# Attention with routed experts on one core: the second half's key sums, moved ahead of the keys' projection

## Chip, cores and metric

The kernel runs on one core of one Trainium2 chip. The metric is the device time of one execution in microseconds (us). Before the change it is 638.71 us, the median of 3 runs (638.54 to 640.49).

## What is computed

The reference is an attention with random features, followed by a mixture of eight experts of which each token uses one (cut):

```python
def _attn_ref(q, k, v, omega):            # 8 batches x 8 heads, 576 tokens, 64 wide; 128 features
    def phi(x):
        h = np.einsum('bhsd,md->bhsm', x, omega) - np.sum(x * x, axis=-1, keepdims=True) / 2.0
        h = h - np.max(h, axis=-1, keepdims=True)
        return np.exp(h) / np.sqrt(m)
    q_p, k_p = phi(q * scale), phi(k * scale)
    kv = np.einsum('bhsm,bhsd->bhmd', k_p, v)
    z = np.sum(k_p, axis=2)
    num = np.einsum('bhsm,bhmd->bhsd', q_p, kv)
    den = np.einsum('bhsm,bhm->bhs', q_p, z)[..., None] + 1e-06
    return num / den

def _moe_ref(x, expert_emb, tau, w1, w2): # 4608 tokens x 512, 8 experts
    ...
    expert_idx = np.argmax(logits, axis=1)
    for e in range(E):
        h = np.maximum(x[mask] @ w1[e], 0.0)
        out[mask] = gate_w[mask, None] * (h @ w2[e])
```

## The kernel before

The work has two stages. The **attention stage** (about the first 220 us) goes through 36 tiles of 128 tokens (`NTILE`), all 8 heads at once; the main loop is `for i in range(NTILE + LAG + 2)`. In its steady part, i = 7 to 35, one iteration handles the keys of tile i and the queries of tile iq = i - 7 (`LAG`), and finishes work of the tiles just before. The **expert stage** (about 220 us to the end) multiplies gathered tokens by expert weights, in products that run one behind the other on TensorE (line 285).

All five engines run in the order in which the program issues its work (`tc.manual_schedule`), so the order of the calls in the loop body is the order on each engine. The heads are kept in two halves a = 0 and a = 1, the lower and the upper 64 partitions of a key or query tile. The helpers that matter here, with their lines:

- `proj` (L374): features before the exponential, for two halves in turns: 8 matmuls into two PSUM banks. The queries go to banks pb3 and pb1, the keys to pb2 and pb0. In the rows its tile form is 64\*128 (64 rows of the array by 128 columns).
- `maxima` (L378, VectorE): the negated row maxima of a bank, `nmk` for keys, `nmq` for queries.
- `feats` (L388, ScalarE): four exponentials, which read the bank and write `ftk` or `ftq`. A bank can be projected into again once its four are done.
- `kvmm` (L406): the key sums of one half, values and counts, 8 matmuls of form 128\*64 into an accumulator `kva`, which collects over the tiles of half a block of tokens. `kv(1)` and `kv(0)` call it for the keys of tile i - 1. `kv_out` (L420, ScalarE) copies finished accumulators to `kvs`, after which they are begun again.
- `qtr` (L462): 16 transposes of the query features into the two banks `nuu`, form 64\*128 like the projections.
- `qcopy` (L467 ScalarE, L469 VectorE): those transposes to SBUF as `qp`.
- `num` (L482): query features times key sums into `nuu`, 32 matmul records of form 128\*64. `num_out` (L495 to L501, VectorE) divides and writes `xr`; `qtr` of the next iteration waits for it, since it writes the same banks.
- `kv_turn`, `kv_turned`, `kv_logits` (L433, L437 VectorE, L444): every fourth or fifth iteration the key sums are transposed and multiplied by the experts' vectors.
- `routed` (L517 to L570): every three tiles the routing, with scatters of rows by GpSimd (L570), one an iteration.

The steady body on TensorE is: query projection, query transposes, key projection, `kv(1)`, `num`, `kv(0)`, and then the next iteration. A value `u` is the tile's place in its block of nine; at u = 4, `kv(0)` and `kv_out` stand directly behind `kv(1)`.

Of the kernel before, what the change touches and what calls it, by code (L numbers as in the profile page):

```python
# [64 lines left out]
def attention_moe(ctx: ExitStack, tc: tile.TileContext, qT, kT, v1, omT, emb, tau, w1q, w2q, xs, out):  # L65
# [114 lines left out]
    def written(w):  # L180

        for o in put + got:
            tc.declare_no_dep(w.ins, o.ins.name, reason="other rows")
        put.append(w)
# [138 lines left out]
    with ExitStack() as c1:  # L323
# [412 lines left out]
        def go(d, *key):  # L736
            for f, *a in d.pop(key, ()):
                f(*a)
# [7 lines left out]
        for i in range(NTILE + LAG + 2):  # L746
            iq = i - LAG
            for n in QLOADS.get(i, () if i >= NTILE else (iq + 2,) if i >= LAG else (i - 4,)):
                loadq(n)
            ahead = i + (4 if i < 2 else 2)  # L750
            if i == 1 or i > 4:
                load(ahead)
            if i in LOADS:
                first_weights(LOADS[i])
            if i == 1 or i >= 4:
                loadv(4 if i == 1 else ahead)
            if i == 1:
                loadv(LAG - 2)
            go(early, i)
            if i == LAG:  # L760
                written(nc.sync.dma_start(xs[DUM : DUM + P, 0:PAY], padrow))
            if i == XLOAD:
                prow = [nc.values_load(
                    firsti[0:1, t : t + 1], engines=[ET.SP], min_val=t * P, max_val=(E - 1) * REG + t * P,
                    skip_runtime_bounds_check_because=WHY) for t in range(NPRE + 1)]
                for t in range(NPRE):
                    xload(t, prow[t], xgp[t])
            ks, qs = i < NTILE, 0 <= iq < NTILE
            st["both"] = ks
            sb, u = divmod(i - 1, TPS)  # L770

            def kv(*halves, b=None):
                if 0 <= i - 1 < NTILE:
                    for a in halves:
                        kvmm(i - 1, a, int(u > 4) if b is None else b)

            turns, done = 0 <= iq - 1 < NTILE, iq - 1 if ks else iq - 2
            sums = 0 <= done < NTILE and i != NTILE
            k0, q1, k1, q0 = ("k", i, 0), ("q", iq, 1), ("k", i, 1), ("q", iq, 0)
            slot = lambda k: go(mid, i, k)  # L780
            if ks and qs:
                if i > LAG:
                    proj(q1 + (3,), q0 + (1,))
                if turns:
                    qtr(iq - 1, *nu)
                maxima(*q1)
                if turns:
                    qcopy(iq - 1, 1)
                    qcopy(iq - 1, 0, True)
                maxima(*q0)  # L790
                go(spare, i, 4)
                feats(*q1)
                feats(*q0)
                proj(k1 + (2,), k0 + (0,))
                maxima(*k1)
                maxima(*k0)
                kv(1)
                if u == 4:
                    kv(0)
                    kv_out(sb, 0)  # L800
                go(spare, i, 3)
                slot(4)
                if sums:
                    num(iq - 1)
                go(spare, i, 0)
                go(spare, i, 1)
                slot(2)
                if u == 4:
                    kv(0, 1, b=1)
                else:  # L810
                    kv(0)
                if sums:
                    num_out(iq - 1)
                feats(*k1)
                feats(*k0)
                slot(0)
                slot(1)
            elif ks:
                for j in KPROJ.get(i, ()):
                    proj(*keys(j))  # L820
                if i == LAG - 1:
                    proj(("q", 0, 1, 3), ("q", 0, 0, 1))
                go(spare, i, 0)
                maxima(*k0)
                maxima(*k1)
                slot(0)
                if i == LAG - 1:
                    kv_out(0, 0)
                    kv_dense(0, 0)
                    for a in range(2):  # L830
                        kvmm(i - 2, a, 1)
                    kv(0, 1)
                    kv_turn(0, 0)
                    emb2()
                else:
                    kv(0, 1)
                slot(1)
                feats(*k0)
                go(spare, i, 1)
                feats(*k1)  # L840
                slot(2)
            else:
                mine, other = ((3, 1), (0, 2))[:: 1 if i % 2 == NTILE % 2 else -1]
                if qs:
                    proj(q1 + (mine[0],), q0 + (mine[1],))
                kv(1)
                go(spare, i, 2)
                slot(3)
                if turns:
                    qtr(iq - 1, *(pb[k] for k in other))  # L850
                kv(0)
                if sums:
                    num(done)
                go(spare, i, 0)
                if i == NTILE + 1:
                    flush()
                if qs:
                    maxima(*q1)
                    maxima(*q0)
                if i > NTILE and turns:  # L860
                    qcopy(iq - 1, 0, True)
                if qs:
                    feats(*q1)
                if i == NTILE:
                    kv_out(sb, 1)
                    qcopy(iq - 1, 0, True)
                if qs:
                    feats(*q0)
                if turns:
                    qcopy(iq - 1, 1)  # L870
                if sums:
                    num_out(done)
                flush()
                filled(1)
                slot(0)
                slot(1)
                filled(FILLS[i] - 1)
                go(spare, i, 1)
                slot(2)
            if sums and done % G == G - 1:  # L880
                g = done // G
                steps = routed(g)
                if g == GPICK:
                    plan = [(ends, i), (mid, i + 1, 2), (mid, i + 1, 1), (spare, i + 2, 0), (mid, i + 2, 0)]
                    plan += [(mid, i + 3, 2), (mid, i + 3, 1)] + [(ends, i + 3 + k) for k in range(3)]
                elif g == NTILE // G - 2:
                    plan = [(ends, i), (ends, i + 1), (ends, i + 1), (spare, i + 2, 0), (mid, i + 2, 0), (mid, i + 2, 1)]
                    plan += [(ends, i + 2), (ends, i + 3), (ends, i + 3)]
                elif i >= NTILE:
                    plan = [(ends, i)] * 3 + [(spare, i + 1, 0), (mid, i + 1, 0), (mid, i + 1, 1)]  # L890
                    plan += [(ends, i + 2 + k) for k in range(3)]
                else:
                    plan = [(ends, i), (mid, i + 1, 2), (mid, i + 1, 1), (spare, i + 2, 0), (mid, i + 2, 0)]
                    plan += [(mid, i + 3, 2)] + [(ends, i + 3 + k) for k in range(3)]
                if NTILE - 3 < i < NTILE:
                    plan[-3:] = [(ends, i + 3), (mid, i + 4, 3), (ends, i + 5)]
                for n, (d, *key) in enumerate(plan):
                    todo = at(d, *key) if key[0] < NTILE + LAG + 2 else behind
                    todo.insert(0 if n == 0 else len(todo), (next, steps, None))
            go(ends, i)  # L900
            if 0 <= i - 1 < NTILE and u in (4, 8):
                b = u // 4 - 1
                if b and ks:
                    kv_out(sb, b)
                k = int(not ks)
                if i + 2 == LAG:
                    todo = (kv_turned, spare, i + 2, 4), (kv_logits, spare, i + 2, 3), (kv_logits_out, mid, i + 2, 4)
                else:
                    kv_dense(sb, b)
                    todo = (kv_turn, spare, i + 2, 3 - k), (kv_turned, mid, i + 2, 4 - k)  # L910
                    todo += (kv_logits, spare, i + 2 + k, 0), (kv_logits_out, mid, i + 2 + k, 0)
                for f, *key in todo:
                    at(*key).append((f, sb, b))
            if i in LOADS:
                n = LOADS[i]
                at(ends, i + 1).append((first_split, n))
                at(early, i + 2).append((first_rest, n))
# [450 lines left out]
```

## Time and profile before

| | before |
|---|---|
| median of 3 runs | 638.71 us |
| the profiled execution: its time | 639.0 us |
| the profiled execution: its span | 637.4 us |
| TensorE (PE) busy | 626.5 us (98%), 6289 matmul records |
| weight loads (PEld) busy | 534.8 us (84%) |
| VectorE (DVE) busy | 499.4 us (78%) |
| ScalarE (ACT) busy | 434.5 us (68%) |
| GpSimd (POOL) busy | 423.1 us (66%) |
| granted TensorE clock, mean | 0.998 |

The end of a matmul in the profile is modelled, so that TensorE looks busy through short pauses; its pauses are better read from the distance between the starts of two neighbouring groups. The time of the profiled execution is 1.6 us above its span, which is what lies ahead of the first and behind the last instruction.

### The profile page before, as it was taken

How to read it: one execution, taken by the hardware profiler on the slowest of the kernel's cores; microseconds unless marked ns; L12 is line 12 of the kernel's file. 1: busy time of each engine (PE TensorE's matmuls, PEld its weight loads, DVE VectorE, ACT ScalarE, POOL GpSimd, SP SyncE). 2: the span in 40 equal slices, each digit the busy share in tenths (PEclk: the TensorE clock that was granted, in tenths of full speed). 3: DMA queues.
4: the chain of work that ended last, by engine and by line, in shares of the span. 5: the costliest groups of instructions: out<-in, count | busy, mean ns of one | idle time of the engine just before them, and what ended most of it. 6: DMA issues, size and time to landing. Idle time of an engine off the chain costs nothing.

```text
span 637.4 us, 19063 instructions
## 1 busy us (share of the span) xinstructions
PE 626.5 (98%) x6289; PEld 534.8 (84%) x6290; DVE 499.4 (78%) x909; ACT 434.5 (68%) x1143; POOL 423.1 (66%) x603
## 2 busy tenths in 40 slices
PE   9999999999999999999999999999999999999996
PEld 8999999988878787888888888888888888888885
DVE  5788888898879846789888798877778787878754
ACT  6989898898998417666666666666575757576640
POOL 3013333455777644569897898879797988797952
PEclk9999999999999999999999999999999999999999
DMA  7755665777782278888869687887878786968631
GB/s 256 216 153 170 210 197 177 226 206 235 250 284 87 101 236 296 249 214 242 244 193 230 208 225 231 201 248 185 242 186 222 216 242 196 234 206 225 195 116 47
DMA packets 143264, 132.20 MB, mean 207 GB/s; under 512 B 107766, under 2 KB 107894, under 8 KB 143168
## 3 DMA queue, kind: packets, MB, share of 16 engines
q1 hardware_dynamic: 136544, 109.96, 61.4%
q0 software_dynamic: 6480, 20.91, 8.4%
q8 instruction: 57, 0.93, 0.6%
q14 instruction: 39, 0.32, 0.2%
q10 hardware_dynamic: 144, 0.07, 0.0%
HBM read 83.78 MB, written 21.97 MB: 166 GB/s over the span
## 4 chain that ended last, share of the span: by engine, by line
PE 70%; ACT 2%; DVE 1%; DMA 1%; issue 0%; POOL 0%; ACTq 0%
PE pb L285 31%; PE po L285 31%; PE pb L374 2%; PE fs_o L285 2%; PE nuu L482 2%; PE fs_a L285 1%; PE pb L267 1%; ACT ftq L388 1%; PE kva L406 1%; DMA qt<-qT 1%; PE pb L462 0%; PE nuu L462 0%; ACT sq L296 0%; DVE xr L501 0%; DVE rt_p L299 0%
## 5 line engine op out<-in xcount | busy, mean ns | idle before, releaser
L240 POOL TENSOR_TENSOR w2l<-raww,w2h 128x256 f32 x128 | 143.6, 1122 | 7.6
L240 POOL TENSOR_TENSOR w1l<-raww,w1h 128x256 f32 (+1 forms) x130 | 114.9, 884 | 14.6 <-DMA xgp<-xs 5.3
L285 PE MATMUL po<-w2h,hh 128*128 (+1 forms) x288 | 112.2, 390 | 0.0
L285 PE MATMUL po<-w2h,hl 128*128 (+1 forms) x288 | 112.1, 389 | 0.0
L285 PE MATMUL po<-w2l,hh 128*128 (+1 forms) x288 | 112.0, 389 | 0.0
L285 PE MATMUL pb<-w1h,xh 128*128 (+1 forms) x280 | 109.4, 391 | 0.1
L285 PE MATMUL pb<-w1h,xl 128*128 (+1 forms) x280 | 109.1, 390 | 0.0
L285 PE MATMUL pb<-w1l,xh 128*128 (+1 forms) x280 | 109.0, 389 | 0.0
L1086 DVE COPY pl<-pb 128x512 uint16<-128x512 uint16 x68 | 46.7, 690 | 55.9 <-ACT pl L1082 53.0
L1082 ACT ACTIVATE pl<-pb 128x512 uint16<-128x512 uint16 x68 | 39.4, 582 | 69.5 <-PE pb L285 61.1
L388 ACT ACTIVATE ftq<-pb,nmq 128x128 f32<-128x128 f32 x288 | 79.7, 432 | 2.2 <-DVE nmq L378 2.2
L388 ACT ACTIVATE ftk<-pb,nmk 128x128 f32<-128x128 f32 x272 | 76.6, 492 | 4.9 <-DVE nmk L378 4.9
L315 POOL DMA_INDIRECT y<-xgp,tail x36 | 44.6, 1240 | 52.0 <-DVE w1h L234 25.3
L1104 DVE COPY wd<-t 128x1024 uint16<-128x1024 uint16 x68 | 67.3, 991 | 1.6 <-DMA t<-pl 1.5
L1120 ACT ACTIVATE hh<-wd 128x1024 fp32r<-128x1024 f32 x34 | 36.1, 1062 | 42.1 <-DVE wd L1104 37.4
L285 PEld LDWEIGHTS po<-w2h,hh 128*128 128x128 f32 x288 | 54.1, 188 | 11.3
L285 PEld LDWEIGHTS po<-w2h,hl 128*128 128x128 f32 x288 | 54.0, 187 | 11.3
L285 PEld LDWEIGHTS po<-w2l,hh 128*128 128x128 f32 x288 | 54.1, 188 | 11.0
L285 PEld LDWEIGHTS pb<-w1h,xl 128*128 128x128 f32 x280 | 52.6, 188 | 11.2 <-DVE xl L269 0.2
L285 PEld LDWEIGHTS pb<-w1h,xh 128*128 128x128 f32 x280 | 52.5, 187 | 11.1 <-ACT tail L1148 0.5
L285 PEld LDWEIGHTS pb<-w1l,xh 128*128 128x128 f32 x280 | 52.6, 188 | 10.8
L1124 DVE SCALAR_TENSOR_TENSOR hl<-wd,hh 128x1024 fp32r<-128x1024 f32 x34 | 54.8, 1611 | 2.9 <-ACT hh L1120 2.3
(342 smaller groups left out, 1257.2 us busy)
## 6 DMA issues: line engine op xcount, KB each, us to landing
raww<-w1q SPq DMA_DIRECT2D x38, 512.0 KB
raww<-w2q SPq DMA_DIRECT2D x38, 512.0 KB
qt<-qT SPq DMA_DIRECT2D x36, 256.0 KB
kt<-kT SPq DMA_DIRECT2D x35, 256.0 KB
xg<-xs SPq DMA_DIRECT2D x23, 260.5 KB
xgp<-xs SPq DMA_DIRECT2D x15, 260.5 KB
rf<-w1q SPq DMA_DIRECT2D x4, 512.0 KB
rf<-w2q SPq DMA_DIRECT2D x4, 512.0 KB
```

What stands on the lines that cost most here:

```text
L240: ils.append(eng.tensor_tensor(at(l, d)[:, c], raw[:, c], at(h, d)[:, c].bitcast(F32), op=ALU.subtract))
L267: nc.tensor.transpose(bank[:, c * P : (c + 1) * P], src[:, o + c * P : o + (c + 1) * P], ident)
L285: done.append(nc.tensor.matmul(dst, x[:, c * P : (c + 1) * P], ws.rearrange("p o f -> p (o f)"), start=(begin and i == 0 and k == 0), stop ...
L315: w = nc.gpsimd.indirect_dma_start(out=out, out_offset=bass.IndirectOffsetOnAxis(ap=(xg[:, DM:] if tail is None else tail)[:, E : E + 1].b ...
L374: nc.tensor.matmul(st["pj" + w, i, a][:, c, :], st[w, i][r, c, :], om[r, :], start=True, stop=True)
L388: nc.scalar.activation(ft[:, h, :], pj[:, h, :], AF.Exp, bias=nm[:, h : h + 1])
L482: nc.tensor.matmul(pn[a][s * D : s * D + D, h, :], st["qp", i, s][:, 2 * h + a, :], kvs[sb, int(u > 4 - s)][:, 4 * a + h, :], start=True, ...
L1082: nc.scalar.activation(planes[1][:, o : o + 512], halved(src)[:, :, 1], AF.Copy)
L1086: nc.vector.tensor_copy(planes[0][:, o : o + 512], halved(src)[:, :, 0])
L1104: nc.vector.tensor_copy(to, src)
L1120: nc.scalar.activation(hh, wd[:, 0:F], AF.Relu)
L1124: nc.vector.scalar_tensor_tensor(hl, wd[:, 0:F], 0.0, hh.bitcast(F32), op0=ALU.max, op1=ALU.subtract)
```

## The change

One call moves three lines up: in iterations 7 to 35, `kv(1)` stands between the query features (behind the query transposes on TensorE) and the key projection, where it stood behind that projection.

```diff
                 go(spare, i, 4)
                 feats(*q1)
                 feats(*q0)
+                kv(1)
                 proj(k1 + (2,), k0 + (0,))
                 maxima(*k1)
                 maxima(*k0)
-                kv(1)
                 if u == 4:
                     kv(0)
                     kv_out(sb, 0)
```

On TensorE, in iteration 8 (`vt7v` and `ftk_1` are the values and the second half's key features of tile 7; `pb_73` and `pb_71` the banks of the key projection; `qp` the query features that `num` multiplies):

```order
 L462 MATMUL nuu<-ident,ftq_1_547 128x64 x2
+L406 MATMUL kva_1_1_490<-vt7v,ftk_1_594 64x65 x8
 L374 MATMUL pb_73<-om,kt_459 128x128
 L374 MATMUL pb_71<-om,kt_459 128x128
...
-L406 MATMUL kva_1_1_490<-vt7v,ftk_1_594 64x65 x8
 L482 MATMUL nuu<-kvs_0_440,qp_0_638 64x73
 L482 MATMUL nuu<-kvs_0_440,qp_1_636 64x73
```

The key sums went from between the key projection and `num` to between the query transposes and the key projection; `num` now follows the projection directly.

On TensorE in iteration 10, where an accumulator is begun anew (with what each instruction waits for; `Activation` is ScalarE):

```order
 L462 MATMUL nuu<-ident,ftq_1_752 128x64 x2
-L374 MATMUL pb_73<-om,kt_606 128x128 [waits DMAHW5_49,Activation_49]
-L374 MATMUL pb_71<-om,kt_606 128x128 [waits Activation_49]
+L406 MATMUL kva_0_1_875<-vt9v,ftk_1_814 64x65 [waits DMAHW2_49,PE_49,Activation_49]
+L406 MATMUL kva_0_1_875<-vt9v,ftk_1_814 64x65 x7
+L374 MATMUL pb_73<-om,kt_606 128x128 [waits DMAHW5_49]
+L374 MATMUL pb_71<-om,kt_606 128x128
```

The wait for ScalarE is now that of the key sums, ahead of the projection, and the projection behind it has none of its own left. Iterations 19 and 28 read the same.

On TensorE in iteration 11, one of those with the transposed key sums (L433):

```order
 L374 MATMUL pb_73<-om,kt_716 128x128
 L374 MATMUL pb_71<-om,kt_716 128x128
-L406 MATMUL kva_0_1_887<-vt10v,ftk_1_928 64x65 x8
 L433 MATMUL pb_74<-ident,xgp_141 128x128 x4
 L482 MATMUL nuu<-kvs_0_440,qp_0_980 64x73
```

The transposes of the key sums now stand directly behind the projection. The rows of VectorE, ScalarE, GpSimd and of the DMA queue on SyncE stand in the order in which they stood.

## Rows read from the trace of the kernel before

**Rows 1.** Busy by stretch: bounds, length, PE, PEld, DVE, ACT, POOL, clock, DMA, GB/s

```profile
20.00:180.00 160.00, 158.57 (x3518) 146.29 (x3516) 137.18 (x326) 142.41 (x512) 67.04 (x191) 1.00 0.68 204
220.00:632.00 412.00, 411.37 (x1838) 339.74 (x1837) 316.46 (x457) 247.70 (x494) 321.15 (x313) 1.00 0.75 214
```

**Rows 2.** The chain that ended last, 160 to 240 us: start, length, what

```profile
180.06 3.63 DMA qt<-qT
```

**Rows 3.** Timeline of PE, iteration 35 and the next: start, length, operation, idle before

```profile
174.01 1.16 PE L374 MATMUL pb<-om,qt 64*128 64x128 f32 x16
175.13 0.71 PE L462 MATMUL nuu<-ident,ftq 64*128 64x64 f32 x16
175.68 1.11 PE L374 MATMUL pb<-om,kt 64*128 64x128 f32 x16
176.72 0.69 PE L406 MATMUL kva<-vt34v,ftk 128*64 128x65 f32 x16
177.24 1.20 PE L482 MATMUL nuu<-kvs,qp 128*64 128x73 f32 x32
...
178.83 1.16 PE L374 MATMUL pb<-om,qt 64*128 64x128 f32 x16
179.92 0.69 PE L406 MATMUL kva<-vt35v,ftk 128*64 128x65 f32 x16
180.66 0.71 PE L462 MATMUL pb<-ident,ftq 64*128 64x64 f32 x16
181.30 0.69 PE L406 MATMUL kva<-vt35v,ftk 128*64 128x65 f32 x16
```

**Rows 4.** Timeline of PE, end of iteration 15 and iteration 16

```profile
65.90 0.69 PE L406 MATMUL kva<-vt14v,ftk 128*64 128x65 f32 x16
66.52 1.16 PE L374 MATMUL pb<-om,qt 64*128 64x128 f32 x16
67.51 0.70 PE L462 MATMUL nuu<-ident,ftq 64*128 64x64 f32 x16
68.06 1.57 PE L374 MATMUL pb<-om,kt 64*128 64x128 f32 x16
...
71.84 0.65 PE L444 MATMUL nuu<-enbd,xgp 128*64 128x16 f32 x16
```

**Rows 5.** Groups by line, PE, 20 to 180 us: busy, mean ns, idle before

```profile
L374 PE MATMUL pb<-om,kt 64*128 64x128 f32 x464 | 37.2, 283 | 0.3 <-ACT ftk L388 0.3
...
L406 PE MATMUL kva<-vt31v,ftk 128*64 128x65 f32 x64 | 2.3, 225 | 0.6 <-ACT kvs L420 0.6
```

**Rows 6.** Timeline of PE, then of ACT, iteration 19

```profile
84.24 0.70 PE L462 MATMUL nuu<-ident,ftq 64*128 64x64 f32 x16
...
84.91 0.79 ACT L420 ACTIVATE kvs<-kva 128x260 f32<-128x260 f32 x2
```

**Rows 7.** The same pair, iteration 10

```profile
35.46 0.71 PE L462 MATMUL nuu<-ident,ftq 64*128 64x64 f32 x16
...
35.80 0.79 ACT L420 ACTIVATE kvs<-kva 128x260 f32<-128x260 f32 x2
```

**Rows 8.** Timeline of DVE, iterations 16 and 8

```profile
71.09 0.69 DVE L437 COPY xgp<-pb 128x512 f32<-128x512 f32 x1 [0.30 <-PE pb L433]
...
29.25 0.17 DVE L495 TENSOR_SCALAR rr<-nuu 128x8 f32<-128x8 f32 x1 [0.21 <-PE nuu L482]
```

**Rows 9.** Timeline of PE, iteration 21

```profile
97.48 0.69 PE L406 MATMUL kva<-vt20v,ftk 128*64 128x65 f32 x16
98.19 1.25 PE L482 MATMUL nuu<-kvs,qp 128*64 128x73 f32 x32
```

**Rows 10.** Timelines of POOL, PE and ACT, iteration 18

```profile
79.04 0.98 POOL L570 DMA_INDIRECT xs<-xr,posi  x1 [0.94 <-DVE sel L530]
...
78.82 0.71 PE L462 MATMUL nuu<-ident,ftq 64*128 64x64 f32 x16
...
80.42 0.60 ACT L467 ACTIVATE qp<-nuu 128x512 f32<-128x512 f32 x1 [0.90 <-PE nuu L462]
```

## The prediction

> **What bounds the kernel.** I read the busy times by stretch first, then the chain that ended last, then the timelines of TensorE against ScalarE and VectorE in single iterations. From 20 to 180 us, where the changed iterations lie, TensorE shows 158.57 of 160 us busy, at full clock, with ScalarE at 142.41 and VectorE at 137.18 [rows 1]: TensorE paces the loop, and two engines are close behind. The expert stage is TensorE alone (411.37 of 412 us). So a microsecond that the loop gains or loses is one of the whole. Where the loop ends, the chain leaves TensorE for a load of queries, issued at 180.06 [rows 2]; the projection that freed its buffer had started at 178.83 and lasted 1.16 [rows 3], so that load starts later if the loop ends later and covers nothing. I carry the loop's difference through in full.
>
> TensorE's modelled ends hide two sorts of pause. One is a **stall of the key projection**: 1.57 us long in iteration 16 [rows 4] against 1.11 in iteration 35 [rows 3], because it writes a bank that ScalarE's last exponentials of the previous keys still read. The other is a **change of tile form**. Projections and query transposes have the form 64\*128, key sums and `num` 128\*64. Where the form stays, neighbours overlap: the key projection starts 0.55 after the transposes (175.13 to 175.68), `num` 0.52 after the key sums (176.72 to 177.24). Where it changes, the next starts later: key sums 0.64 after transposes (180.66 to 181.30) [rows 3], a projection 0.62 after key sums (65.90 to 66.52) [rows 4].
>
> **The change, part by part.**
>
> *Order.* The key sums are moved out of a row of like form into the middle of another, so that an iteration has four changes of form instead of two. Before, from the transposes to `num`: 0.55 + 1.04 + 0.52 = 2.11 [rows 3]. After, from the same view: transposes to key sums 0.64, key sums to projection 0.62, and a projection entered from key sums and left to key sums 1.09 (178.83 to 179.92), taken for the unseen step from projection to `num`, which has the key sums' form: 2.35. `num` itself lasts 1.20 when it follows key sums at once [rows 3] and 1.25 when its stream starts afresh [rows 9]. Together 0.24 + 0.05 = 0.29, in 29 iterations **+8.4**. The bounds: at least the bare difference 0.64 - 0.55 = 0.09 for each of two added changes, 29 x 0.18 = +5.2; at most, if the unseen step cost another such 0.09, +11.0. I take 8.4, since all but that one step is a row.
>
> [...]
>
> *Stalls.* The key projections are busy for 37.2 us and idle ahead of them for 0.3 [rows 5]; 29 at 1.11 would be 32.2, so stalls are 37.2 + 0.3 - 32.2 = 5.3 us. With the key sums ahead, a projection comes 0.64 + 0.62 = 1.26 after the transposes instead of 0.55, 0.71 later, and the stall of 0.46 in iteration 16 is covered. The key sums need only the second half's features, which ScalarE makes before the first half's. **-5.3**. They now wait for each head's exponential by itself; those are done by then, so I cost these waits at nothing. The key tile's buffer comes free 0.7 later, which its next load, more than an iteration ahead of its use, covers.
>
> *A new wait.* In iterations 10, 19 and 28 the key sums begin an accumulator anew and must wait for ScalarE to copy the old one out (L420), and the key projection now stands behind that wait. In iteration 19 they could start at 84.24 + 0.64 = 84.88; the copies end at 84.91 + 0.79 = 85.70, a wait of 0.82 [rows 6]. In iteration 10 it is 36.59 - 36.10 = 0.49 [rows 7]; I take 28 like 10. That makes 1.8, less 0.3 in each of 10 and 28, since the iteration before has made TensorE later by its 0.29 and ScalarE not: **+1.2** (bounds 0 to 1.8).
>
> *Late maxima.* VectorE takes the key maxima behind the key projection. That ends at 175.68 + 1.11 = 176.79 in iteration 35 and would end at 175.13 + 1.26 + 1.16 = 177.55; in stalled iteration 16 at 69.63 before, 67.51 + 2.42 = 69.93 after. So these maxima come 0.3 to 0.8 later. In the iterations with transposed key sums VectorE had 0.30 idle before the copy L437 [rows 8], behind which L444 waits (71.84, rows 4 show it starting as that copy ends, 71.09 + 0.69 = 71.78). There the 0.46 - 0.29 that TensorE wins is lost again: 5 iterations x 0.2 = 1.0. In plain ones only 0.21 was idle before `num_out` [rows 8]; I estimate that 0.1 more than TensorE's own delay reaches the next transposes, in seven of them, 0.7. Iteration 32 wins nothing from its filled stall, since behind it TensorE waits 0.6 for ScalarE anyway [rows 5]; half of that I give back, 0.3. **+2.0** (bounds 0 to 4).
>
> *Cover.* Where `num` waits for the query copies, the added time is partly free: in iteration 21 it starts 0.71 after the key sums [rows 9] instead of 0.52. Where the transposes wait for VectorE too: 1.12 after the query projection in iteration 35 (174.01 to 175.13) [rows 3] against 0.99 in 16 (66.52 to 67.51) [rows 4]. I estimate eight such places at 0.16: **-1.3**.
>
> **Sum.** 8.4 - 5.3 + 1.2 + 2.0 - 1.3 = **+5.0**. The profiled execution took 639.0 us with a span of 637.4; it becomes 644.0. The median is 0.3 below it (638.7), so I forecast 643.7. A measurement tells about 0.3% (1.9 us) from no change.
>
> **The rivals.**
> - *No change.* VectorE and ScalarE keep up: the new wait and the late maxima cost nothing, leaving 8.4 - 5.3 - 1.3 = +1.8, 640.5; with the changes of form at their lower bound 5.2 it is -1.4, 637.3. For it: both engines are idle about a tenth of the loop. Against it: their idle time does not lie at these places [rows 6, 8]. Chance 0.16.
> - *Faster.* The weight loads of the next group slip under the running matmuls in the new order too, and a change of form costs what the like-form step shows beyond the stream itself, some 0.06 an iteration: 1.7 - 5.3 - 1.3 = -4.9, 633.8. It decides itself at the step from transposes to key sums: at 0.55 instead of 0.64 this case holds. All the steps that I see speak against it. Chance 0.05.
> - *Much slower.* In iteration 18 a GpSimd scatter runs from 79.04 to 80.02; the transposes end inside it at 79.53, but ScalarE's copy, released by them, starts only at 80.42 [rows 10]: the release came 0.4 after the scatter's end. If the key projection's end, now later, falls into the scatter of the iterations that follow such a one, and is held alike, VectorE gets its maxima about 1.0 later in seven iterations: +7 on top, 650.7. Against it: that end would fall only some 0.3 into the scatter, and I see no projection held. A partial hold is in my range. Chance 0.12.
>
> The forecast's own case has the remaining 0.67.
>
> **Numbers.** Its own range is 640.5 to 647 (order cost 5.2 to 11.0, not at both ends with the rest). The range that leaves out little over 1 in 10 is 639.2 to 648.5. Slower by over 0.3% (above 640.6): the main case almost whole, the much slower one, and a little of the first rival, 0.80. Within: 0.14. Faster: 0.06.
>
> **What would show it.** Right: the key projection's groups all near 1.16 us long; transposes to key sums 0.64, projection to `num` 1.09; a wait of the key sums for L420 in iterations 10, 19 and 28; VectorE idle before `nmk`; the loop's end some 5 us later and the expert stage as long as before. Wrong: steps of 0.55 at the new borders (faster), key projections still stalled (ScalarE later than I think), or VectorE's maxima starting 1 us behind the projection's end (held release).

## The result and the profile after

| | before | changed |
|---|---|---|
| median, same chip | 639.87 us (638.54 to 640.49, 6 runs) | 643.74 us (642.99 to 644.20, 6 runs) |
| the profiled execution: its time / its span | 639.0 / 637.4 us | 643.67 / 642.0 us |

The ratio is 1.0061, 95% interval 1.0041 to 1.0081: **slower by 3.9 us**. The forecast was 643.7 us, 5.0 above the 638.71 from which I started; between the two profiled executions the difference is 4.7. (That the absolute figure fits to 0.1 is partly luck: with all six runs the kernel before took 639.87 and not 638.71.)

The page of the change, its busy times over the whole span:

```profile
PE 628.5 (98%) x6289; PEld 533.6 (83%) x6290; DVE 500.6 (78%) x909; ACT 435.6 (68%) x1143; POOL 423.5 (66%) x603
```

The same instructions, and 4.6 us more of span. Where these lie shows in TensorE's timeline. The end of iteration 35 and what follows, in the change (start, length, operation):

```profile
179.71 0.71 PE L462 MATMUL nuu<-ident,ftq 64*128 64x64 f32 x16
180.35 0.69 PE L406 MATMUL kva<-vt34v,ftk 128*64 128x65 f32 x16
180.97 1.16 PE L374 MATMUL pb<-om,kt 64*128 64x128 f32 x16
182.06 1.25 PE L482 MATMUL nuu<-kvs,qp 128*64 128x73 f32 x32
183.14 0.63 PE L406 MATMUL kva<-vt34v,ftk 128*64 128x65 f32 x16
183.70 1.16 PE L374 MATMUL pb<-om,qt 64*128 64x128 f32 x16
```

The loop's last border, the projection that started at 178.83 [rows 3], now starts at 183.70. Read in the same way at iteration 8 (24.76 before, 24.57 after), the loop takes 159.13 us in place of 154.07: **+5.06**. From that border to the end of the span it is 458.5 before and 458.3 after. So the whole loss arises in the loop, and none of it is covered later. (These are 28 of the 29 changed iterations; iteration 7 is 0.14 longer.)

From the transposes to `num` it is 182.06 - 179.71 = 2.35 where it was 2.11 [rows 3], in steps of 0.64, 0.62 and 1.09, and `num` lasts 1.25 instead of 1.20: the forecast's 0.29, to the hundredth. The groups of TensorE from 20 to 185 us in the change (busy, mean ns | idle before), against [rows 5]:

```profile
L374 PE MATMUL pb<-om,kt 64*128 64x128 f32 x464 | 33.7, 285 | 0.0
...
L444 PE MATMUL nuu<-enbd,xgp 128*64 128x16 f32 x112 | 4.5, 212 | 0.6
...
L406 PE MATMUL kva<-vt31v,ftk 128*64 128x65 f32 x64 | 2.5, 226 | 0.8 <-ACT kvs L420 0.8
```

The key projections fell from 37.2 busy and 0.3 idle to 33.7 and none. That is 29 x 1.16: **not one is stalled**. In exchange there is idle time ahead of L444, and more ahead of the key sums of iteration 32 (the last line, 0.6 before). Iteration 16 in the change, TensorE and then VectorE:

```profile
69.18 0.69 PE L462 MATMUL nuu<-ident,ftq 64*128 64x64 f32 x16
69.81 0.69 PE L406 MATMUL kva<-vt15v,ftk 128*64 128x65 f32 x16
70.42 1.16 PE L374 MATMUL pb<-om,kt 64*128 64x128 f32 x16
71.64 0.63 PE L433 MATMUL pb<-ident,xgp 128*128 128x128 f32 x4
72.20 1.25 PE L482 MATMUL nuu<-kvs,qp 128*64 128x73 f32 x32
73.55 0.65 PE L444 MATMUL nuu<-enbd,xgp 128*64 128x16 f32 x16
```

```profile
71.61 1.29 DVE L378 TENSOR_REDUCE nmk<-pb 128x4 f32<-128x512 f32 x2 [0.35 <-PE pb L374]
72.82 0.68 DVE L437 COPY xgp<-pb 128x512 f32<-128x512 f32 x1
```

The projection is 1.16 long instead of 1.57 [rows 4]. But the maxima begin at 71.61, only as it ends, the copy L437 follows them without the 0.30 of idle time that it had [rows 8], and L444 starts as that copy ends (72.82 + 0.68 = 73.50). The iteration takes 0.05 more than before, where the filled stall alone would have made it 0.17 shorter (0.46 - 0.29).

The new wait, TensorE in iterations 28 and 29 of the change:

```profile
138.55 0.69 PE L406 MATMUL kva<-vt27v,ftk 128*64 128x65 f32 x16 [0.82 <-ACT kvs L420]
...
143.59 0.71 PE L462 MATMUL nuu<-ident,ftq 64*128 64x64 f32 x16 [0.53 <-DVE xr L501]
```

and in iterations 10 and 19:

```profile
36.65 0.69 PE L406 MATMUL kva<-vt9v,ftk 128*64 128x65 f32 x16 [0.36 <-ACT kvs L420]
...
87.21 0.69 PE L406 MATMUL kva<-vt18v,ftk 128*64 128x65 f32 x16 [0.16 <-ACT kvs L420]
```

By the starts, the distance from the last transpose to the first key projection is 0.77 in every other iteration, and 1.20, 1.00 and 1.66 in these three: waits of 0.43, 0.23 and 0.89.

By iteration, from one query projection's start to the next, the change against before: +0.28 to +0.30 in 12, 17, 24, 33 and 35, where nothing had stalled; -0.22 to +0.05 in 16, 19, 22, 31 and 34, whose key projection had; +0.02 to +0.20 in 15, 21, 23, 26 and 30, whose key projection had not either; +0.59 in 10, +0.83 in 28, +0.57 in 29 and +0.38 in 27.

### The profile page after: what moved, and what is told of

Same layout as the page of the kernel before. It is cut to its first block, busy times and chain, and to the rows that moved or that the text cites. A ratio compares the mean times of both kernels' runs of the same rounds, so it can differ in the third digit from the quotient of the medians.

```text
span 642.0 us, 19060 instructions
## 1 busy us (share of the span) xinstructions
PE 628.5 (98%) x6289; PEld 533.6 (83%) x6290; DVE 500.6 (78%) x909; ACT 435.6 (68%) x1143; POOL 423.5 (66%) x603
## 4 chain that ended last, share of the span: by engine, by line
PE 69%; ACT 2%; DVE 2%; issue 1%; POOL 0%; ACTq 0%
PE pb L285 31%; PE po L285 31%; PE fs_o L285 2%; PE pb L374 1%; PE nuu L482 1%; ACT ftq L388 1%; PE fs_a L285 1%; PE pb L267 1%; PE kva L406 0%; PE pb L462 0%; DVE nmq L378 0%; ACT qp L467 0%; DVE xr L501 0%; ACT sq L296 0%; DVE rt_p L299 0%
```

## Experiments

They ran on three chips. On the first (e1 to e4) the kernel before took 635.73 us beside them, on the second (c1, c2, e5, e6) 638.59, on the third (e7 to e9, c3) 635.18. That difference turned out to be part of the answer, so loops (from iteration 8's to iteration 36's query projection) are compared with a trace of before from a chip of the same sort. In kernels with a table at the top all lines are one further down (L407 is L406).

**What the waits for L420 cost (e1): the old order in iterations 10, 19 and 28 alone.**

```diff
-                kv(1)
+                if u > 0:
+                    kv(1)
                 proj(k1 + (2,), k0 + (0,))
                 maxima(*k1)
                 maxima(*k0)
+                if not (u > 0):
+                    kv(1)
```

> The change, except in iterations 10, 19 and 28, which begin an accumulator and keep the old place of the key sums. Theory (there the moved sums wait for ScalarE's copies L420 with the key projection behind them; the change's trace shows those iterations and the next longer by 0.59 + 0.15, 0 and 0.83 + 0.57 us than before): 1.5 to 2.0 us less than the change, about 642.0 us; the step from transposes to key projection in all other iterations stays 0.77. Rival (ScalarE is late there anyway, so the old order stalls its projection by as much): at most 0.5 us less than the change.

Measured 640.2 us, ratio 1.0068 [1.0045, 1.0090]; loop 156.39. TensorE in its iteration 28:

```profile
135.28 0.69 PE L462 MATMUL nuu<-ident,ftq 64*128 64x64 f32 x16
135.81 1.11 PE L374 MATMUL pb<-om,kt 64*128 64x128 f32 x16
136.85 0.69 PE L406 MATMUL kva<-vt27v,ftk 128*64 128x65 f32 x16
137.37 1.20 PE L482 MATMUL nuu<-kvs,qp 128*64 128x73 f32 x32
```

No wait is left; the three take 4.74, 4.67 and 4.67 us instead of 5.46, 5.20 and 5.87. The change itself did not run on this chip, but e4 did, which has the new order in all iterations; there the three take 1.76 us more than in e1. Of that, 3 x 0.29 = 0.87 is the order, which e1 gives back there too, and 0.89 the waits (0.43, 0.23 and 0.23 in e4 by the starts).

**The order's price by itself (e2): the new order in seven iterations that had no stall.**

```diff
+PLAIN = (12, 15, 17, 24, 27, 33, 35)
...
+                if i in PLAIN:
+                    kv(1)
                 proj(k1 + (2,), k0 + (0,))
                 maxima(*k1)
                 maxima(*k0)
-                kv(1)
+                if not (i in PLAIN):
+                    kv(1)
```

> The kernel before, with the key sums moved ahead in seven iterations alone (12, 15, 17, 24, 27, 33, 35), whose key projection does not stall and which begin no accumulator. Theory (the two added changes of tile form cost 0.29 us an iteration where there is nothing to fill): +1.9 to +2.3 us over the kernel before, each of the seven longer by 0.2 to 0.4 and the others as they were. Rival (the loss of the change is made by late maxima on VectorE and by the waits for L420, not by the order on TensorE): within 0.5 us of the kernel before.

Measured 637.0 us, ratio 1.0015 [0.9996, 1.0034], +1.3 us and by itself too little to tell. Its trace tells more: against c3 (before, on a chip of this sort) six of the seven are longer by 0.29 or 0.30, the seventh, 27, whose projection was stalled by 0.25 in c3, by 0.03; their sum is 1.79, and the whole loop is 2.13 longer. Iteration 12 of e2:

```profile
46.55 0.71 PE L463 MATMUL nuu<-ident,ftq 64*128 64x64 f32 x16
47.20 0.69 PE L407 MATMUL kva<-vt11v,ftk 128*64 128x65 f32 x16
47.81 1.16 PE L375 MATMUL pb<-om,kt 64*128 64x128 f32 x16
48.90 1.25 PE L483 MATMUL nuu<-kvs,qp 128*64 128x73 f32 x32
```

2.35 again, with nothing stalled, waiting or late around it: this is the price of the order and of nothing else. One surprise: the stalls of the *untouched* iterations 16, 19, 22, 31 and 34 were gone too, though their order was the old one.

**Do GpSimd's scatters make the stalls (e3, e4)?** Both kernels with each scatter issued later, behind VectorE's copy of the next transposes.

```diff
-                o = nc.vector.tensor_copy(qp, st["tr", i][s])
+                o = st["dv"] = nc.vector.tensor_copy(qp, st["tr", i][s])
...
-                tc.add_manual_dep(w.ins, st["out"].ins.name, sync, reason="one scatter a tile")
+                tc.add_manual_dep(w.ins, (st["dv"] if st["both"] else st["out"]).ins.name, sync, reason="one scatter a tile")
...
+                plan = [(spare, key[0] + 1, 4) if n > len(plan) - 4 and d is ends and key[0] + 1 < NTILE else (d, *key)
+                        for n, (d, *key) in enumerate(plan)]
```

> The kernel before, with each routing scatter issued half an iteration later, behind VectorE's copy of the query transposes, so that it no longer runs while the transposes end. Theory (a scatter holds TensorE's release of the transposes by up to 0.9 us in about seven iterations, which makes ScalarE late and the next key projection stall): the 0.4 us stalls of iterations 16, 19, 22, 25, 31 and 34 go, 2 to 4 us less than before, about 637 us. Rival (ScalarE's own load makes the stalls): within 0.7 us of before, stalls of the key projection as long as before (37.2 us busy in the group).

> The change, with the same later scatters. Theory (the change has no stalls left, so that their cause going away gives it little): 0 to 1.0 us less than the change, about 643 us, which makes the new order 5.5 to 7.5 us dearer than the old one with later scatters. Rival (the change's loss comes with the held releases): within 2 us of the old order with later scatters.

Measured 635.93 us for e3, ratio 1.0012 [0.9983, 1.0041], and 645.47 for e4, 1.0134 [1.0097, 1.0172]. e3's loop takes 151.0, 3.1 less than in the first trace of before, which looks like the gain. It proves nothing: e2 showed the same stalls gone on this chip with the scatters where they were. And both lose 3 to 4 us behind the loop (461.6 and 462.7 from its end on, against 458.5), of which more at e7; the twelve executions of e3 spread from 633.57 to 640.98, and the trace is one of 638.55. Inconclusive.

**Both kernels once more (c1 before, c2 the change), on another chip.**

> The kernel before, profiled on the chip of the runs beside it. Theory (the trace before has releases held behind the scatters, the runs e1 to e3 have none, so this is a matter of chip and run and not of the order): where no release of the transposes comes more than 0.2 us late, the projection's stalls of iterations 16, 19, 22, 25, 31 and 34 shrink from 0.46 to 0.1 us or less and iterations 8 to 35 take some 3 us less than in the first trace (154.1 us). Rival (the moved sums of e2 made those stalls go): stalls and length as in the first trace.

> The change on the same chip. Theory (order cost 0.29 us in each of 29 iterations, whatever the stalls): beside a kernel before without held releases it is the dearer, since there are fewer stalls to fill: 5 to 7 us over it; beside one with held releases 3.5 to 5 us. Rival (the change costs the same whatever is held): 3.5 to 4.5 us in either case.

c1 639.07 us, ratio 1.0004 [0.9990, 1.0018], loop 154.15; c2 643.44, ratio 1.0073 [1.0054, 1.0093], loop 159.01. Here the stalls of the old order are back (projections 1.30 to 1.32 from first to last start in 16, 19, 22, 28, 31 and 34), and so is the pattern of the first pair, but for 27 and 28: +4.9 in the loop.

**A move that crosses no change of form (e5): `kv(1)` directly behind `num`, from the kernel before.**

```diff
-                kv(1)
+                if u == 4 or not sums:
+                    kv(1)
...
+                    if u != 4:
+                        kv(1)
```

> The kernel before with the second half's key sums moved the other way, behind num (not at u = 4), within the row of operations that have the same tile form. Theory (a move that adds no change of tile form costs TensorE nothing): steps 0.55 from transposes to projection and 1.04 from projection to num; num and num_out come 0.5 us earlier, so that the transposes wait less for VectorE; 0 to 2 us less than before. Where the copies of the query transposes are held, num waits for them: then up to 2 us more. Rival (any move of these sums makes VectorE and ScalarE late): 2 us or more over before without held releases.

Measured 643.68 us, ratio 1.0086 [1.0067, 1.0106], +5.1. That is more than I expected, a miss for the total. In iterations 8, 9, 17, 26 and 35, where `num` does not wait, the period is the same as before to 0.01, so a move inside a row of like form is free by itself. But iteration 15 of e5 shows what the key sums had hidden:

```profile
62.95 1.12 PE L374 MATMUL pb<-om,kt 64*128 64x128 f32 x16
64.53 1.25 PE L482 MATMUL nuu<-kvs,qp 128*64 128x73 f32 x32 [0.46 <-DVE qp L469]
```

`num` waits for the query copies. In 15, 18, 21, 24, 27, 30 and 33 this costs 0.35 to 0.76 each, and the iterations with L444 0.16 to 0.68. The key sums in their old place were the cover of those copies. (On this chip those copies come late, see c3; e5 did not run on one where they do not.)

**The late maxima (e6): the change with the old order in the six iterations of the transposed key sums.**

```diff
+TURNS = (11, 16, 20, 25, 29, 34)
...
-                kv(1)
+                if i not in TURNS:
+                    kv(1)
                 proj(k1 + (2,), k0 + (0,))
                 maxima(*k1)
                 maxima(*k0)
+                if not (i not in TURNS):
+                    kv(1)
```

> The change, with the old order in the six iterations 11, 16, 20, 25, 29 and 34, which transpose the key sums (L433, L437, L444). Theory (there the late key maxima push VectorE's copy L437 and with it L444, on top of the order cost): 1.2 to 1.8 us less than the change; those iterations shorter by 0.15 to 0.32 each. Rival (VectorE has room there; only order cost less the stall comes back): 0.2 to 0.8 us less.

Measured 641.68 us, ratio 1.0039 [1.0024, 1.0055], 1.76 less than c2 on the same chip; the six iterations are shorter by 0.33, 0.13, 0.33, 0.12, 0.31 and 0.03, or 1.25 together. The time is as expected, but three of the six gain less than the 0.15 that I had as the least. Nor is the 1.25 the price of late maxima alone: the old order also takes back its own 6 x 0.29 = 1.74, and in 16, 25 and 34 stalls return (0.22, 0.22 and 0.46).

**The scatters once more, in the loop alone (e7 old order, e8 new order), both sorts of waits taken out (e9), and before beside them (c3).** e7 and e8 have the edit of e3 with `key[0] + 1 < 29`, which leaves the last scatters in place. e9 is e6 with `if i not in TURNS and u > 0`.

> The kernel before, unchanged, for a trace from the chip of the three kernels beside it. It tells whether held releases occur there: with them the loop from iteration 8 to 36 takes about 154.1 us, without them 151 to 152.5, and the time is 638.5 to 640 or about 636.

> The kernel before, with each of the loop's scatters (up to iteration 28) issued a little later, behind VectorE's copy of the next query transposes, and the last ones where they were. Theory (the stalls of the old order come from query copies whose release is held by a scatter that runs when the transposes end): on a chip where the kernel before shows held releases (late query copies in iterations 15, 18, 21, 24), the loop from iteration 8 to 36 goes from about 154.1 to 151.0 to 152.0 us and the time is 2 to 3 us below before; on a chip without them, within 1 us of before. Rival (the stalls come from ScalarE being full, whatever the scatters do): loop 153.5 to 154.5 on a chip with holds and no gain. In either case the end part stays as in before, without the 3 us that the earlier kernel with all scatters late lost there.

> The changed kernel with the same late scatters. Theory: the new order has no stalls left that a held release causes, so the scatters' place is worth at most 1 us to it: loop 158.0 to 159.2, time 3.5 to 5.0 us above before on a chip with held releases, 6 to 8 above on one without; and 5.5 to 7.5 us above the old order with late scatters on the same chip, whatever the chip. Rival (the new order has held releases of its own that cost it): 2 us or more below the change, loop below 157.

> The changed kernel with the old order in the nine iterations where waits were seen: 10, 19 and 28 (accumulators begun anew) and 11, 16, 20, 25, 29, 34 (transposed key sums). Theory (the two costs are separate and add): 1.8 for the turns and 2.7 for the new sums below the change, less up to 0.5 since iteration 29 is in both: loop 154.8 to 155.8. On a chip where the kernel before has held releases that is 0.5 to 1.5 us above before, on one without 3.5 to 4.5 above. Rival (the nine waits share one cause, TensorE running ahead of VectorE, and one repair gives most of both): loop 156.3 or more.

| on the third chip | time, us | ratio | loop, us |
|---|---|---|---|
| c3, before | 634.99 | 1.0004 [0.9986, 1.0021] | 150.79 |
| e7, old order, late scatters | 638.64 | 1.0051 [1.0035, 1.0068] | 150.61 |
| e8, new order, late scatters | 646.33 | 1.0173 [1.0149, 1.0197] | 157.74 |
| e9, new order outside nine iterations | 638.91 | 1.0065 [1.0044, 1.0086] | 154.71 |

*c3* is the instructive one: the unchanged kernel, 4.1 us faster than on the second chip, and 3.4 of that in the loop. Iteration 18 of c3, on TensorE, GpSimd and ScalarE:

```profile
78.45 0.71 PE L462 MATMUL nuu<-ident,ftq 64*128 64x64 f32 x16
```

```profile
78.67 0.98 POOL L570 DMA_INDIRECT xs<-xr,posi  x1 [0.94 <-DVE sel L530]
```

```profile
79.20 0.60 ACT L467 ACTIVATE qp<-nuu 128x512 f32<-128x512 f32 x1
```

The scatter starts 0.22 behind the transposes, exactly as in [rows 10] (78.82 and 79.04). The query copy starts 0.75 behind them, where it had been 1.60. So on this chip the copy is released on time beside a scatter, and on the first measurement's chip it was held. In the trace of before, seven scatters of the loop run as transposes end: VectorE's query copy starts 1.07 to 1.61 behind the transposes' start in six of these iterations (15, 18, 21, 24, 30 and 33), and at most 0.98 in 27 and in all iterations without such a scatter. In the change it is six of seven again, now with 27 and without 18; on the first and third chips it is none. That points to the scatter, but no run moved it on a chip with holds: that it is the cause is argued and not shown. Without a hold, iteration 19's key projection takes 0.84 between its first and last start instead of 1.30, and all key projections together 35.0 us instead of 37.2:

```profile
L374 PE MATMUL pb<-om,kt 64*128 64x128 f32 x464 | 35.0, 281 | 0.3 <-ACT ftk L388 0.3
```

So 2.2 of the 5.3 us of stalls come and go with the held releases, by one program on two sorts of chip.

*e7 and e8* leave the loop almost as it was (150.61 against 150.79; e8 157.74 against e4's 158.01), as they should on a chip without holds. Whether late scatters would help on one with holds was not tried. Their times miss what I expected, by some 3 us, and the loss lies behind the loop. VectorE and GpSimd in e7:

```profile
191.14 3.31 DVE L532 TENSOR_TENSOR sel<-iotm,mx 128x24 bf16<-128x24 f32 x1
```

```profile
191.12 0.19 POOL L490 COPY xr<-ids 128x1 int32<-128x1 int32 x1
191.24 0.44 POOL L529 COPY xr<-raw 128x8 f32<-128x8 f32 x3
191.65 2.75 POOL L617 TENSOR_TENSOR w2l<-rf,w2h 128x256 fp32r<-128x256 f32 x4
```

and in c3:

```profile
192.13 0.19 DVE L532 TENSOR_TENSOR sel<-iotm,mx 128x24 bf16<-128x24 f32 x1
```

```profile
192.10 0.25 POOL L490 COPY xr<-ids 128x1 int32<-128x1 int32 x1
192.23 0.48 POOL L529 COPY xr<-raw 128x8 f32<-128x8 f32 x3
192.63 2.80 POOL L617 TENSOR_TENSOR w2l<-rf,w2h 128x256 fp32r<-128x256 f32 x4
```

The same VectorE instruction takes 0.19 us in c3, where GpSimd's copy beside it is the one that is longer (0.25), and 3.31 in e7, where it ends only when GpSimd's whole row has ended (194.45 and 194.40). TensorE waits 2.49 for it. In e3, e4 and e8 it takes 3.30 or 3.31 as well, in the ten other traces 0.19 or 0.20. What decides is not shown: GpSimd's copy starts first in all fourteen, by 0.01 to 0.03, but the four are just those with late scatters.

The wait is not the whole loss. Behind it TensorE's clock falls; e7, from 195 to 197 us and later (bounds, length, PE, PEld, DVE, ACT, POOL, clock, DMA, GB/s), and the instruction ahead of the second stretch:

```profile
195.00:197.00 2.00, 2.00 (x11) 1.35 (x11) 1.93 (x7) 1.92 (x8) 0.00 (x0) 0.50 0.01 2
...
255.21 0.47 PE L285 MATMUL pb<-w1h,xh 128*128 x1 [2.95 <-DVE w1l L232]
...
257.00:260.00 3.00, 3.00 (x10) 2.27 (x9) 1.58 (x2) 2.63 (x3) 0.00 (x0) 0.53 1.01 379
```

c3 has a granted clock of 1.00 in both stretches, as the first trace of before has. In e8, behind the same wait, it is 0.50 to 0.53 from 203 to 210 us, and 0.66 on average from 200 to 210. The second wait is in e7 alone, whose trace is the slowest of its six executions (641.88): from the loop's end on it takes 465.7 us, c3 457.9.

*e9* comes close to what its theory said: loop 154.71, and 3.7 us above before. Iteration by iteration it differs from e8 in 10, 19 and 28 (0.72, 0.53, 0.54: 1.8 us), in the six turns (0.16, 0.33, 0.29, 0.33, 0.01, 0.32: 1.4) and by -0.19 in 32. The two savings are separate and add. Neither is the price of waits alone: with the nine iterations e9 also leaves out their order, 9 x 0.29 = 2.6 of the 3.2, as far as nothing covers it. What stays, 3.9 us of loop over c3, is the order where it is kept: +0.29 or +0.30 in 12, 15, 17, 21, 24, 26, 30, 33 and 35, and +0.10 to +0.25 in iterations whose old projection was a little long.

**No kernel here beats the one before.**

## Why the prediction was right, and where not

- **Order, +8.4.** Right: 0.29 in an iteration, as summed from rows of before, in after, c2, e2, e8 and e9 alike. The step that had no row, projection to `num`, is the 1.09 that I took for it. The bounds 5.2 and 11.0 were both far off. e2 (+0.29 for two added changes) and e5's move inside a row of like form (period the same to 0.01) agree that it is the change of form that costs, 0.145 us each.
- **Stalls, -5.3.** Right in size: 37.5 to 33.7 us of key projection, and 33.7 holds 29 x 0.05 that belong to the order. What I said of their cause (ScalarE's last exponentials) was only the last link. By c3, 2.2 us of them are there only where query copies are late, which happens beside scatters.
- **New wait, +1.2.** Total about right, 0.43 + 0.23 + 0.89 = 1.55, but by luck, since no part is: I had 0.19, 0.82 and 0.19. In 10 I took off 0.3, but iteration 9 was longer by 0.13 only, since it had a short stall to fill. In 19 I took the 0.82 of before; but there the copy L420 ended late because iteration 18's query copy had been held, and in the change it is not. In 28 I took iteration 10's 0.19, and the change brought a hold there. TensorE, GpSimd and ScalarE in iterations 27 and 28 of the change:

```profile
131.64 0.71 PE L462 MATMUL nuu<-ident,ftq 64*128 64x64 f32 x16
...
131.87 0.99 POOL L570 DMA_INDIRECT xs<-xr,posi  x1 [0.94 <-DVE sel L530]
...
133.20 0.60 ACT L467 ACTIVATE qp<-nuu 128x512 f32<-128x512 f32 x1 [1.33 <-PE kva L406]
...
137.70 0.80 ACT L420 ACTIVATE kvs<-kva 128x260 f32<-128x260 f32 x2
```

  The transposes of iteration 27 started at 131.64 and their copy only at 133.20. On chips without holds the wait in 28 is 0.23, as in 19 (e4, e8). The steps that failed are the 0.82 taken over for 19 from before, and "I take 28 like 10".
- **Late maxima, +2.0.** Right in kind. Iteration 16 from `num` to the next query projection, before and then in the change:

```profile
70.76 1.25 PE L482 MATMUL nuu<-kvs,qp 128*64 128x73 f32 x32
71.84 0.65 PE L444 MATMUL nuu<-enbd,xgp 128*64 128x16 f32 x16
...
72.92 1.16 PE L374 MATMUL pb<-om,qt 64*128 64x128 f32 x16
```

```profile
72.20 1.25 PE L482 MATMUL nuu<-kvs,qp 128*64 128x73 f32 x32
73.55 0.65 PE L444 MATMUL nuu<-enbd,xgp 128*64 128x16 f32 x16
...
74.64 1.16 PE L374 MATMUL pb<-om,qt 64*128 64x128 f32 x16
```

  That step is 2.43 or 2.44 in all six iterations with transposed key sums, and was 2.11 to 2.27: 1.6 together, of which 0.3 is `num`'s own 0.05, so 1.3 for the late copy L437 where I had priced 1.0 in five. (e6 and e9 are no second measure of it, since they give back the order as well.) The 0.7 for plain iterations did not come: 0.29 or 0.30 is all that they show. Not foreseen was iteration 29 (+0.57), where the transposes wait for VectorE after 28's late start. In 32 nothing was gained (7.34 before, 7.36 after): its stall of 0.74 gave way to a longer wait for L420, and I had given back only 0.3.
- **Cover, -1.3.** Right in size, in other places than I named. In 21 and 30, where `num` had waited for a held copy, the order costs 0.04 and 0.02 instead of 0.29; 15 and 23 show 0.20 and 0.15. In 26 and 28 the key sums behind `num` had been long before (0.92 and 0.91, against 0.65 and 0.63 in the change), which I did not see; these two come out 0.27 below the other terms each. The six make 1.3. The step of 1.12 into iteration 35's transposes, which I read as a wait, is 1.13 in the change too and covered nothing.
- **Sum.** 28 x 0.29 - 5.2 + 1.6 + 1.3 = 5.8 for order, stalls, waits and the late copy, and the loop shows 5.06. The rest, -0.7, is the cover of 1.3 less 0.5 in 32 and some 0.1 in other places. It is bookkeeping: each stall is put in at its full length.
- **The rivals.** *Faster* fell at the step that it named, 0.64 and not 0.55. *No change* needed free waits and maxima, and they cost 1.55 and 1.3. *Much slower* needed a key projection held for about 1 us; in the change VectorE's maxima start as the projection ends (71.61, iteration 16), and in none of the 28 iterations is an idle VectorE held by more than a quarter of a microsecond.

What I did not see: that the answer depends on the chip. Where query copies come late, the old order loses 3.3 us in the loop by c3 and the new one about 1.4 (159.13 against 157.74 in e8, whose scatters are late). So on a chip without holds I expect the change to be dearer. e8 against e7 says 7.1 us of loop; the change itself was not run there.

## What to carry to other kernels

Count the changes of tile form along TensorE's row before moving a block of matmuls, and price them by the distance between starts at a border that the trace already shows; a move inside a row of like form was free in e5 where nothing waited (the period was the same to 0.01 us), but take care what the moved block was covering. A stall removed by a later start is worth its full length only where the engines behind it have idle time at that place: here VectorE's maxima and ScalarE's copies took back 1.3 and 1.55 of the 5.3 us, more than half. And compare on chips of one sort: the same kernel differed by 4 us between chips, as much as the change is worth.

## What the runs showed of the hardware

- On some chips who waits for TensorE's transposes starts late when a GpSimd scatter of about 1.0 us runs as they end: the query copy of iteration 18 started 1.60 us after the transposes' start, 0.40 after the scatter's end; on others 0.75, with the scatter at the same place. It is so at six of seven such scatters in before and in the change each; that the scatter is the cause is not shown by a run. The kernel before takes 638.6 to 639.9 us on the former chips and 635.0 to 635.7 on the latter. Why chips differ in this is open.
- Two more changes of tile form on TensorE cost 0.29 us an iteration where nothing else interfered, so 0.145 each, in c2, e2, e8 and e9 as in the change.
- A VectorE instruction (L532) of 0.19 us in c3 took 3.31 in e7, beside a row of eight GpSimd instructions, which overlap: it started 0.02 after the first of them (191.12 and 191.14) and ended 0.05 after the last (194.40 and 194.45). The order of starts does not tell the two apart: GpSimd's copy starts first in c3 too (192.10 and 192.13), and there VectorE takes 0.19. The long form, 3.30 or 3.31, is in the four traces with late scatters alone; why is not shown.
- After TensorE had waited 2.49 us, its granted clock was 0.50 from 195 to 197 us in e7, and 1.00 in c3 and in the first trace of before, which have no such wait.
